# Attention scores against block keys: one matmul for both query halves, and another form of filler matmul

## The chip, the cores and the metric

One core of a Trainium2 chip runs the whole program. Its TensorE (PE in the rows) multiplies a stationary matrix, loaded as weights (PEld), with a stream of moving columns and writes to PSUM. VectorE (DVE), ScalarE (ACT) and GpSimd (POOL) work on PSUM and SBUF, and SyncE (SP) issues the loads and stores. The metric is the device time of one execution in microseconds (us). Three runs of the kernel before took 647.77, 648.09 and 649.55 us; their median is 648.09.

## What is computed

Three stages follow each other. The first is attention with 2 batches of 8 heads, 768 positions and 64 dimensions a head. Every query sees the keys that lie less than 16 positions away, and besides them 24 block keys, one for each block of 32 positions (the maximum over the block's keys; its value is the block's mean). The second and third are two feed-forward networks on the 1536 x 512 result.

```python
k_sum = k.reshape(B, H, nb, block, D).max(axis=3)      # nb = 24 blocks of 32
v_sum = v.reshape(B, H, nb, block, D).mean(axis=3)
scores_l = scale * np.matmul(q, k.transpose(0, 1, 3, 2))        # masked to |i - j| < 16
scores_s = scale * np.einsum('bhsd,bhnd->bhsn', q, k_sum) + np.log(block)
a = softmax(concat([masked scores_l, scores_s]))
x = a @ concat([v, v_sum])
# then
x = rmsnorm(x) * rms_g ; x = (silu(x @ w_gate) * (x @ w_val)) @ w_out
out = (s * relu(x @ w_in)**2 + b) @ w_out2
```

## The kernel before, in words

The queries are cut into 12 tiles of 128 positions, 6 for each batch. A head pair (NPAIR = 4 of them) lies on the 128 partitions: head g = 0 on partitions 0 to 63, head g = 1 on 64 to 127, with the 64 dimensions of a head as rows. A tile's 128 queries are two halves of 64, c = 0 and c = 1, since each half has a window of KW = 96 keys of its own: its 64 positions and 16 on either side. The NS = 24 block keys (`km`) are the same for both halves. So the scores of one head and one tile are 128 queries x KC = 120 columns, 96 of the window and 24 of the blocks, and four heads of them fill one PSUM bank; `box["S", i, g]` is the bank of tile i and of the heads g of all four pairs.

`do_qk` (L510 to L523) writes the scores of a tile. For each pair j it issues four matmuls of 64 x 64 weights and 96 columns for the window, one for each (g, c), and then four of 64 x 64 weights and 24 columns for the block keys. The queries are the weights, with 64 rows (the dimensions of one head) and 64 columns (the queries of one half); the output goes to partitions 0 to 63 or 64 to 127 of the bank. All operands are float32, and each such matmul appears in the profile as two rows, two passes; a tile of scores is 4 x 8 x 2 = 64 rows of L522.

After the scores, VectorE adds the mask and takes the minimum of the negated scores (`do_top`, L541), ScalarE exponentiates (L548), TensorE transposes the result (L559), ScalarE copies it to SBUF (L569), and TensorE multiplies with the values (L578, 120 x 64 weights, 66 columns). Norms, another transposition (L627) and the split of x into a high and a low part (L638, L640) follow. The block keys come from L284, the block sums of the values from L294, their transposition from L299.

The order of this stage is made by a planner, `give_out` (L328 to L417). It goes through a model of time with a cost for each task (1.25 us for a tile's scores, 0.44 for four transposes), and issues on each engine the first task by rank whose inputs are there in the model. Where the model's TensorE would stand idle for more than IDLE = 0.6 us, it issues a filler into a free PSUM bank: four transposes of the identity matrix (L413 and L414), which the model counts as 0.44 us and whose result nobody reads. The first matmuls of the feed-forward network (L726, L727, L730, in the halves and in float32r) are tasks of the same planner; from some 115 us on the plain loops of `moe` run. The order that the planner finds is what the program has; on the chip each engine goes through its own list and waits on semaphores.

Of the kernel before, what the change touches and what calls it, by code (L numbers as in the profile page):

```python
# [24 lines left out]
NS = SEQ // BLK  # L25
HQ = 64
VH = 66
KW = HQ + 2 * WIN
KC = KW + NS
# [13 lines left out]
QB = 3  # L43
# [11 lines left out]
def kernel(ctx: ExitStack, tc: tile.TileContext, q_t, k_t, v_w, v_t, w_gate, w_val, w_out, w_in2, w_out2, vecs, out):  # L55
    nc = tc.nc
# [40 lines left out]
    def bank(i):  # L97
        return psp.tile([128, 512], F32, tag=f"b{i}", name=f"b{i}")


    ident = const.tile([128, 128], F32, name="ident")
# [7 lines left out]
    qc = [const.tile([128, NPAIR, 2, HQ], F32, name=f"q{i}") for i in range(QB)]  # L109
# [13 lines left out]
    kst = [t[:, 0:NPAIR * KL].rearrange("p (j s) -> p j s", j=NPAIR) for t in kb]  # L123
    vst = [[t.rearrange("p (s h d) -> p s h d", s=NTL, h=NH) for t in ts]
           for ts in ([t[:, 0:VT] for t in vb], [part[:, i * VT:(i + 1) * VT] for i in range(2)])]
    km = [const.tile([128, NPAIR, NS], F32, name=f"km{b}") for b in range(NB)]
# [192 lines left out]
    def task(eng, us, fn, deps=(), rank=0.0, take=(), give=(), bank=None, free=(), more=0.09):  # L319

        t = dict(eng=eng, us=us, fn=fn, deps=[d for d in deps if d is not None], rank=rank, take=take, give=give,
                 bank=bank, free=free, more=more, end=None)
        tasks.append(t)
        return t
# [3 lines left out]
    def give_out():  # L328
        count = {k: 0 for k in rings}
        freed = {k: 0 for k in rings}  # L330
        done_at = {k: [] for k in rings}
        bank_free = [(0.0, i) for i in range(8)]
        used_caps = {k: [] for k in caps}
        pending = {e: [] for e in ("PE", "DVE", "ACT", "POOL", "SP")}
        for i, t in enumerate(tasks):
            pending[t["eng"]].append((t["rank"], i, t))
        for p in pending.values():
            p.sort(key=lambda z: z[:2])
        clock = dict.fromkeys(pending, 0.0)
        dma = 0.0  # L340
        now = 0.0
        left = len(tasks)

        ends = {k: {} for k in rings}

        def ring_ok(k):
            n = rings[k]
            c = count[k]
            return c < n or (c - n in ends[k] and ends[k][c - n] <= now)

        while left:
            moved = False
            for e in ("SP", "PE", "ACT", "DVE", "POOL"):
                if clock[e] > now + 1e-9:
                    continue
                for z in pending[e]:
                    t = z[2]
                    if any(d["end"] is None or d["end"] + LAT > now + 1e-9 for d in t["deps"]):
                        continue
                    if not all(ring_ok(k) for k in t["take"]):  # L360
                        continue
                    b = None
                    if t["bank"]:
                        if sum(1 for x in used_caps[t["bank"]] if x["freed"] is None or x["freed"] > now) >= caps[t["bank"]]:
                            continue
                        ok = [x for x in bank_free if x[0] <= now]
                        if not ok:
                            continue
                        b = min(ok)
                        bank_free.remove(b)  # L370
                        t["b"] = b[1]
                        t["freed"] = None
                        used_caps[t["bank"]].append(t)
                    t["slot"] = {}
                    for k in t["take"]:
                        t["slot"][k] = count[k]
                        count[k] += 1
                    if e == "SP":
                        dma = max(dma, now + 0.5) + t["us"]
                        clock[e] = max(now + 0.06, dma - AHEAD)  # L380
                        t["end"] = dma + 1.3
                    else:
                        clock[e] = now + t["us"]
                        t["end"] = clock[e] + (0.06 if e == "PE" else t["more"])
                    for k, o in t["give"]:
                        ends[k][o["slot"][k]] = t["end"] + LAT
                    for o in t["free"]:
                        o["freed"] = t["end"] + LAT
                        bank_free.append((o["freed"], o["b"]))
                    t["at"] = now  # L390
                    if b is not None:
                        t["fn"](b[1])
                    else:
                        t["fn"]()
                    pending[e].remove(z)
                    left -= 1
                    moved = True
                    break
            if moved:
                continue  # L400
            nxt = [c for c in clock.values() if c > now + 1e-9]
            nxt += [x[0] for x in bank_free if x[0] > now]
            nxt += [v for k in rings for v in ends[k].values() if v > now]
            nxt += [t["end"] + LAT for t in tasks if t["end"] is not None and t["end"] + LAT > now + 1e-9]
            assert nxt, [z[2]["why"] if "why" in z[2] else (e, z[0]) for e in pending for z in pending[e][:3]]
            now = min(nxt) + 1e-6
            at = clock["PE"] + IDLE
            if now > at and any(x[0] <= at for x in bank_free) and ident_at[0]["end"] is not None and ident_at[0]["end"] + LAT < at and pending["PE"]:

                now = at  # L410
                i = min(bank_free)[1]
                ps = bank(i)
                for k in range(4):  # L413
                    nc.tensor.transpose(ps[:, k * 128:(k + 1) * 128], ident, ident)  # L414
                clock["PE"] = now + 0.44

    def dve(n):  # L417
        return 0.07 + 1.042e-3 * n
# [10 lines left out]
    def plan(x):  # L429
# [12 lines left out]
        def lq(i, rank, deps=()):  # L442
            Q[i] = task("SP", mb(128 * 512 * 4), lambda: load_q(i), deps, rank=rank)
# [60 lines left out]
        box = {}  # L504
        def tile_of(n, i):
            b, t = divmod(i, NTL)
            if i >= 2:
                lq(i, n - 5, [qk[i - QB]] if i >= QB else ())

            def hold(bk):  # L510
                box["S", i, 0] = bank(bk)

            def do_qk(bk):
                box["S", i, 1] = bank(bk)
                sm_of[i] = smallp.tile([128, 2, NH], F32, tag="sm", name="sm")
                four = [(g, c) for g in range(2) for c in range(2)]
                for j in range(NPAIR):
                    for o, n in ((0, KW), (KW, NS)):
                        for g, c in four:
                            p = slice(64 * g, 64 * g + 64)  # L520
                            k0 = 64 * (2 * t + c)
                            nc.tensor.matmul(box["S", i, g][64 * c:64 * c + 64, j * KC + o:j * KC + o + n], qc[i % QB][p, j, c],  # L522
                                             km[b][p, j] if o else kst[b][p, j, k0:k0 + KW], start=True, stop=True)  # L523
            deps = [Q[i], *[KM[b, j] for j in range(NPAIR)], *([qk[i - 1]] if i else ())]
            A0 = task("PE", 0.0, hold, deps, n + 1.2, bank="S")
            A1 = qk[i] = task("PE", 1.25, do_qk, [*deps, A0], n + 1.2, bank="S", take=("sm",))
            box["A0", i] = A1
            return A0, A1

        for n, (i, g) in enumerate(us):  # L530
            b, t = divmod(i, NTL)
# [86 lines left out]
            S = task("POOL", 0.75, do_ss, [R], n - 2)  # L618
# [50 lines left out]
        for s in range(NSUB):  # L669
            for j in range(HEAD):  # L670
                rk = FR[s] + j * FS
                got = {}
                for k in range(2):
                    ps = []
# [38 lines left out]
                c = task("DVE", dve(512), lambda f=do_v: f(0), [b_, got[1][2]], rr, free=(got[1][0],))  # L713
# [153 lines left out]
    x = [xs0]  # L867
    plan(x)
    give_out()
    n = 2 * HEAD + MORE  # L870
    prog[:] = [n, n, n, n]
# [71 lines left out]
```

## Time and profile before

| | |
|---|---|
| median of three runs | 648.09 us |
| the profiled execution's own time | 647.01 us |
| its span, first to last instruction | 645.2 us |
| TensorE busy | 622.8 us, 97% of the span, 3816 matmul rows |
| VectorE, ScalarE, GpSimd busy | 378.1, 259.8, 141.7 us |
| mean granted TensorE clock | 0.992 |
| score matmuls, 96 columns (384 rows) | 277 ns mean of one |
| score matmuls, 24 columns (384 rows) | 208 ns mean of one |
| filler transposes (52 rows) | 327 ns mean of one |

A row's duration is its latency, from the start to the last result, and rows overlap: eight rows of 24 columns that take some 0.2 us each are through in 0.08 us. What a group costs TensorE is therefore read from start to start, not from the durations. "Busy" of an engine in a stretch is the part of it in which at least one of its rows runs. The column PEclk is the granted clock of TensorE as a share of full speed (1.00 is 2.4 GHz, 0.50 is 1.2 GHz). In the chain of waits "issue" is time in which an engine waited for nothing that the profile shows.

### The profile page before, as it was taken

How to read it: one execution, taken by the hardware profiler on the slowest of the kernel's cores; microseconds unless marked ns; L12 is line 12 of the kernel's file. 1: busy time of each engine (PE TensorE's matmuls, PEld its weight loads, DVE VectorE, ACT ScalarE, POOL GpSimd, SP SyncE). 2: the span in 40 equal slices, each digit the busy share in tenths (PEclk: the TensorE clock that was granted, in tenths of full speed). 3: DMA queues.
4: the chain of work that ended last, by engine and by line, in shares of the span. 5: the costliest groups of instructions: out<-in, count | busy, mean ns of one | idle time of the engine just before them, and what ended most of it. 6: DMA issues, size and time to landing. Idle time of an engine off the chain costs nothing.

```text
span 645.2 us, 9632 instructions
## 1 busy us (share of the span) xinstructions
PE 622.8 (97%) x3816; PEld 514.3 (80%) x3816; DVE 378.1 (59%) x731; ACT 259.8 (40%) x524; POOL 141.7 (22%) x159
## 2 busy tenths in 40 slices
PE   5588999999999999999999999999999999999998
PEld 3576788888888888888888888888888888888886
DVE  5469886325851555544556767870388457845532
ACT  2576986334433333212333345542554045404400
POOL 2253856322311111111111111100221022103100
PEclk9889999999999999999999999999999999999999
DMA  9979622003440112221122212230212321210022
GB/s 294 230 264 257 193 60 74 1 1 98 131 130 28 42 63 66 86 61 53 62 65 69 64 65 67 65 100 31 56 46 67 94 62 42 66 61 0 2 98 99
DMA packets 17494, 55.04 MB, mean 85 GB/s; under 512 B 2000, under 2 KB 2256, under 8 KB 17448
## 3 DMA queue, kind: packets, MB, share of 16 engines
q1 hardware_dynamic: 17448, 54.42, 27.7%
q8 instruction: 30, 0.49, 0.3%
q14 instruction: 16, 0.13, 0.1%
HBM read 50.35 MB, written 3.15 MB: 83 GB/s over the span
## 4 chain that ended last, share of the span: by engine, by line
PE 91%; DVE 3%; issue 2%; DMA 1%; ACT 1%; SPq 0%; POOL 0%; POOLq 0%
PE b L726 22%; PE b L730 22%; PE b L727 22%; PE b L852 7%; PE b L850 7%; PE b L849 7%; PE b L559 2%; PE b L522 2%; PE b L578 2%; DMA vt<-in_v_t_dram 1%; PE b L627 1%; DVE vt L294 1%; DVE P L541 0%; DVE km L284 0%; ACT P L548 0%
## 5 line engine op out<-in xcount | busy, mean ns | idle before, releaser
L231 POOL TENSOR_TENSOR wl<-wa,wh 128x512 fp32r<-128x512 f32 x68 | 89.1, 1318 | 389.3 <-ACT wh L227 316.0
L726 PE MATMUL b<-x,wh 128*128 128x512 f32 x288 | 113.7, 395 | 0.1
L727 PE MATMUL b<-x,wl 128*128 128x512 f32 x288 | 112.2, 390 | 0.0
L227 ACT ACTIVATE wh<-wa 128x512 fp32r<-128x512 f32 x68 | 41.5, 627 | 97.2 <-PE b L852 45.5
L730 PE MATMUL b<-x,wh 128*128 128x512 f32 x288 | 77.8, 392 | 0.0
L850 PE MATMUL b<-wl,hg 128*128 128x512 f32 (+1 forms) x196 | 75.1, 385 | 0.0
L849 PE MATMUL b<-wh,hg 128*128 128x512 f32 (+1 forms) x196 | 75.1, 385 | 0.0
L726 PE MATMUL b<-y,wh 128*128 128x512 f32 x192 | 74.7, 389 | 0.0
L727 PE MATMUL b<-y,wl 128*128 128x512 f32 x192 | 74.7, 389 | 0.0
L831 DVE SCALAR_TENSOR_TENSOR b<-u,vec 128x512 f32<-128x512 f32 x48 | 50.7, 1057 | 35.6 <-ACT u L830 35.6
L726 PEld LDWEIGHTS b<-x,wh 128*128 128x128 f32 x288 | 54.1, 188 | 11.3 <-ACT x L638 0.4
L727 PEld LDWEIGHTS b<-x,wl 128*128 128x128 f32 x288 | 54.1, 188 | 10.7
L730 PEld LDWEIGHTS b<-x,wh 128*128 128x128 f32 x288 | 53.5, 188 | 11.0
L726 PE MATMUL b<-hg,wh 128*128 128x512 f32 x144 | 56.0, 389 | 0.0
L727 PE MATMUL b<-hg,wl 128*128 128x512 f32 x144 | 56.0, 389 | 0.0
L751 DVE SCALAR_TENSOR_TENSOR hg<-b,vec,hg 128x512 fp32r<-128x512 f32 x48 | 36.0, 749 | 28.1 <-ACT hg L750 28.1
L852 PE MATMUL b<-wh,hg 128*128 128x512 f32 (+1 forms) x196 | 51.5, 385 | 0.0
L730 PE MATMUL b<-y,wh 128*128 128x512 f32 x192 | 51.3, 389 | 0.0
L216 DVE SCALAR_TENSOR_TENSOR wa<-raw,wa 128x512 int32<-128x512 int32 x68 | 50.0, 735 | 2.0
L750 ACT ACTIVATE hg<-b,vec 128x512 fp32r<-128x512 f32 x48 | 33.0, 687 | 43.0 <-DVE b L831 43.0
L858 DVE TENSOR_TENSOR part<-b,part 128x512 f32<-128x512 f32 (+1 forms) x37 | 24.4, 673 | 43.5 <-PE b L852 43.5
L215 DVE SCALAR_TENSOR_TENSOR wa<-raw,wa 128x512 int32<-128x512 int32 x68 | 47.0, 691 | 2.0
(85 smaller groups left out, 947.2 us busy)
## 6 DMA issues: line engine op xcount, KB each, us to landing
raw<-in_w_out_dram SPq DMA_DIRECT2D x28, 512.0 KB, 3.5
raw<-in_w_in_dram SPq DMA_DIRECT2D x16, 512.0 KB, 4.1
raw<-in_w_gate_dram SPq DMA_DIRECT2D x12, 512.0 KB, 3.6
raw<-in_w_val_dram SPq DMA_DIRECT2D x12, 512.0 KB, 3.6
hg<-in_k_t_dram SPq DMA_DIRECT2D x8, 400.0 KB, 10.0
q<-in_q_t_dram SPq DMA_DIRECT2D x12, 256.0 KB, 7.1
vt<-in_v_t_dram SPq DMA_DIRECT2D x8, 384.0 KB, 8.3
out_dram<-part SPq DMA_DIRECT2D x11, 256.0 KB, 2.0
```

The source lines that it names most:

```text
L215: lambda: nc.vector.scalar_tensor_tensor(out=ai, in0=hi, scalar=-0x80000000, in1=ai, op0=ALU.bitwise_and, op1=ALU.bitwise_or),
L216: lambda: nc.vector.scalar_tensor_tensor(out=ai, in0=lo, scalar=29, in1=ai, op0=ALU.logical_shift_right, op1=ALU.bitwise_or),
L227: nc.scalar.activation(out=r(h), in_=a_t[i], func=AF.Copy)
L231: nc.gpsimd.tensor_tensor(out=r(lo), in0=a_t.pop(i), in1=high[i], op=ALU.subtract)
L726: nc.tensor.matmul(ps, r(hi[:, kk * 128:(kk + 1) * 128]), xh, start=kk == 0, stop=False)
L727: nc.tensor.matmul(ps, r(lo[:, kk * 128:(kk + 1) * 128]), xh, start=False, stop=False)
L730: nc.tensor.matmul(ps, r(hi[:, kk * 128:(kk + 1) * 128]), r(act(kk, 1)), start=False, stop=kk == 3)
L751: nc.vector.scalar_tensor_tensor(out=r(dst[1]), in0=ps, scalar=bias, in1=dst[0], op0=ALU.add, op1=ALU.subtract)
L831: after(0, lambda u=u, ps=ps: nc.vector.scalar_tensor_tensor(out=ps, in0=u, scalar=sbc[:, 0:1], in1=u, op0=ALU.mult, op1=ALU.mult))
L849: nc.tensor.matmul(acc, gh, r(ws[e][0][:, cs]), start=e == 0, stop=False)
L850: nc.tensor.matmul(acc, gh, r(ws[e][1][:, cs]), start=False, stop=False)
L852: nc.tensor.matmul(acc, r(ge[e][:, 1]), r(ws[e][0][:, cs]), start=False, stop=e == 3)
```

## The change

There are two edits. The scores of the block keys are no longer computed once for each half of the queries: the two halves of a head stand side by side as 128 columns of one set of weights (64 rows x 128 columns), and one matmul of 24 columns writes all 128 partitions of the bank. A pair then has four window matmuls of 64 x 64 as before, and two block matmuls of 64 x 128, so a tile has 4 x (8 + 4) = 48 rows for 64. A filler is one float32 matmul of the identity with 256 columns, the identity taken twice, in place of four transposes: two rows for four. The planner's costs are as before, so its order is as before.

```diff
@@ give_out
                 ps = bank(i)
-                for k in range(4):
-                    nc.tensor.transpose(ps[:, k * 128:(k + 1) * 128], ident, ident)
+                nc.tensor.matmul(ps[:, 0:256].rearrange("p (o c) -> p o c", o=2), ident, ident.rearrange("p (o c) -> p o c", o=1).broadcast_to([128, 2, 128]), start=True, stop=True)
                 clock["PE"] = now + 0.44
@@ do_qk
-                four = [(g, c) for g in range(2) for c in range(2)]
                 for j in range(NPAIR):
-                    for o, n in ((0, KW), (KW, NS)):
-                        for g, c in four:
-                            p = slice(64 * g, 64 * g + 64)
+                    for g in range(2):
+                        p = slice(64 * g, 64 * g + 64)
+                        S = box["S", i, g]
+                        for c in range(2):
                             k0 = 64 * (2 * t + c)
-                            nc.tensor.matmul(box["S", i, g][64 * c:64 * c + 64, j * KC + o:j * KC + o + n], qc[i % QB][p, j, c],
-                                             km[b][p, j] if o else kst[b][p, j, k0:k0 + KW], start=True, stop=True)
+                            nc.tensor.matmul(S[64 * c:64 * c + 64, j * KC:j * KC + KW], qc[i % QB][p, j, c], kst[b][p, j, k0:k0 + KW], start=True, stop=True)
+                    for g in range(2):
+                        p = slice(64 * g, 64 * g + 64)
+                        nc.tensor.matmul(box["S", i, g][:, j * KC + KW:(j + 1) * KC], qc[i % QB][p, j].rearrange("p c q -> p (c q)"), km[b][p, j], start=True, stop=True)
```

The lists of VectorE, ScalarE, GpSimd and SyncE hold the same instructions in the same order before and after; on TensorE 96 places and 13 fillers differ. The first place is on TensorE, in the tile of scores that stands behind 69 us between two halves of a feed-forward matmul (in the kernel before it starts at 86.35 us). A row gives the line, the operation, the tile written, the tiles read, and weight columns x moving columns; `hg` holds the keys, `q` the queries, x2 stands for the two halves. Before:

```order
L726 MATMUL b_1377<-x,wh 128x512
L727 MATMUL b_1377<-x,wl 128x512
L522 MATMUL b_1376<-hg,q_100 64x96 x2
L522 MATMUL b_1392<-hg,q_100 64x96 x2
L522 MATMUL b_1376<-km_110,q_100 64x24 x2
L522 MATMUL b_1392<-km_110,q_100 64x24 x2
L522 MATMUL b_1376<-hg,q_100 64x96 x2
```

The same place after:

```order
L727 MATMUL b_1258<-x,wh 128x512
L728 MATMUL b_1258<-x,wl 128x512
L521 MATMUL b_1257<-hg,q_100 64x96 x2
L521 MATMUL b_1273<-hg,q_100 64x96 x2
L524 MATMUL b_1257<-km_110,q_100 128x24
L524 MATMUL b_1273<-km_110,q_100 128x24
L521 MATMUL b_1257<-hg,q_100 64x96 x2
```

The window matmuls stand where they stood; behind them come two block matmuls of 128 weight columns instead of four of 64, in each of the four pairs.

The second place is on TensorE too, between the scores of tile 0 and those of tile 1: the first four fillers, the transposes of tile 0 (`P`), and those of the value sums (`vt`). Before:

```order
L522 MATMUL b_155<-km_109,q_99 64x24 x2
L414 MATMUL b_193<-ident 128x128 x4
L414 MATMUL b_206<-ident 128x128 x4
L414 MATMUL b_216<-ident 128x128 x4
L414 MATMUL b_229<-ident 128x128 x4
L559 MATMUL b_237<-ident,P 120x128 x4
L559 MATMUL b_243<-ident,P 120x128 x4
L299 MATMUL b_250<-ident,vt 128x128 x4
```

The same place after:

```order
L524 MATMUL b_155<-km_109,q_99 128x24
L413 MATMUL b_185<-ident 128x256
L413 MATMUL b_195<-ident 128x256
L413 MATMUL b_202<-ident 128x256
L413 MATMUL b_212<-ident 128x256
L560 MATMUL b_217<-ident,P 120x128 x4
L560 MATMUL b_223<-ident,P 120x128 x4
L299 MATMUL b_230<-ident,vt 128x128 x4
```

Each filler is one matmul in place of four transposes, and nothing else moved.

## Rows read from the trace of the kernel before

**Rows 1.** Windows: busy us (xinstructions) of PE, PEld, DVE, ACT, POOL; PEclk, DMA, GB/s

```profile
42.00:69.00 27.00, 22.89 (x381) 18.50 (x381) 25.87 (x68) 20.13 (x53) 13.70 (x18) 1.00 0.79 216
69.00:645.00 576.00, 573.04 (x2960) 474.05 (x2960) 330.44 (x568) 220.34 (x418) 115.73 (x104) 1.00 0.21 64
```

**Rows 2.** Chain that ended last, in order of time: start us, us, what

```profile
20.60 2.25 issue
...
28.26 4.58 issue
...
40.70 0.84 issue
...
69.00 0.69 PE b L578 x16
```

**Rows 3.** Windows between the stops, columns as in rows 1

```profile
0.00:20.61 20.61, 13.30 (x222) 10.20 (x222) 11.46 (x35) 6.88 (x16) 4.87 (x25) 1.00 0.93 288
...
22.85:28.29 5.44, 5.41 (x125) 4.86 (x126) 2.86 (x22) 3.03 (x10) 0.94 (x4) 0.69 1.04 169
...
32.84:40.71 7.87, 7.65 (x126) 6.40 (x125) 4.78 (x26) 6.08 (x19) 3.63 (x6) 0.74 1.03 387
```

**Rows 4.** DMA queues, 30 to 32 us: packets, MB, share of engines

```profile
q8 instruction: 1, 0.02, 4.2%
```

**Rows 5.** Page, part 3: DMA queues, whole span

```profile
q8 instruction: 30, 0.49, 0.3%
```

**Rows 6.** Windows around the slow clock, columns as in rows 1

```profile
23.26:26.67 3.41, 3.41 (x60) 3.02 (x56) 2.13 (x17) 1.79 (x5) 0.32 (x2) 0.50 1.08 171
...
30.08:36.91 6.83, 4.06 (x35) 3.48 (x35) 2.02 (x11) 2.28 (x7) 1.01 (x1) 0.50 1.03 327
```

**Rows 7.** Windows, line L522 alone: us, PE, PEld, PEclk, DMA, GB/s

```profile
69.00:115.00 46.00, 5.40 (x256) 4.98 (x256) 1.00 0.30 90
```

**Rows 8.** Timeline of PE, one tile: start us, us, what, shape, type, count

```profile
85.80 0.39 PE L726 MATMUL b<-x,wh 128*128 128x512 f32 x1
86.02 0.40 PE L727 MATMUL b<-x,wl 128*128 128x512 f32 x1
86.35 0.40 PE L522 MATMUL b<-hg,q 64*64 64x96 f32 x8
86.57 0.26 PE L522 MATMUL b<-km,q 64*64 64x24 f32 x8
86.65 0.38 PE L522 MATMUL b<-hg,q 64*64 64x96 f32 x8
...
87.41 0.26 PE L522 MATMUL b<-km,q 64*64 64x24 f32 x8
87.60 0.50 PE L726 MATMUL b<-x,wh 128*128 128x512 f32 x1
87.94 0.40 PE L727 MATMUL b<-x,wl 128*128 128x512 f32 x1
```

**Rows 9.** Timeline of PEld, same place, columns as in rows 8

```profile
85.80 0.19 PEld L727 LDWEIGHTS b<-x,wl 128*128 128x128 f32 x1
86.35 0.15 PEld L522 LDWEIGHTS b<-hg,q 64*64 64x64 f32 x4 [0.36 <-issue]
```

**Rows 10.** Line L414, the fillers: ns min/median/max, first and last start

```profile
L414 PE MATMUL b<-ident x52: 272/273/474, 10.1 to 70.0; 128*128 128x128 f32 x52
```

**Rows 11.** Timeline of PE, first stage

```profile
14.87 1.81 PE L559 MATMUL b<-ident,P 128*120 128x128 f32 x8
16.52 0.60 PE L299 MATMUL b<-ident,vt 128*128 128x128 f32 x4
...
25.63 0.60 PE L522 MATMUL b<-hg,q 64*64 64x96 f32 x8
...
37.24 0.40 PE L522 MATMUL b<-hg,q 64*64 64x96 f32 x8
```

**Rows 12.** Timeline of ACT: the last exponentials of tile 1

```profile
20.79 1.81 ACT L548 ACTIVATE P<-P,sm 128x120 f32<-128x120 f32 x6
```

## The prediction

> **What bounds the kernel now.** I read the stretches first. From 69 us to the end TensorE is the bound: it is busy for 573.04 of the 576 us there, VectorE for 330.44 [rows 1]. Whatever the change adds to TensorE's own work behind 69 us is added to the time. From 42 to 69 us VectorE is the bound (25.87 of 27 us), and TensorE stands idle for 4.1 [rows 1]. Before 42 us I read the chain of waits. Beside loads it holds three stops of TensorE that no semaphore ends, put down to "issue": 2.25 us at 20.60, 4.58 at 28.26, 0.84 at 40.70 [rows 2]. Their places tell what they are. TensorE ran 222 matmul rows up to the first, 125 from there to the second, 126 to the third [rows 3]. Each row is a weight load and a matmul, so the stops lie some 250 instructions apart. A packet of the instruction queue moves between 30 and 32 us, shortly ahead of the end of the longest stop [rows 4], and the queue's packets are some 16 KB each (0.49 MB in 30) [rows 5]; the DMA engines are full meanwhile (shares of 0.93 to 1.04) [rows 3]. So I read the stops as TensorE waiting for its own code behind the loads. The stops also cost clock: the granted clock was 0.50 from 23.26 to 26.67 and from 30.08 to 36.91, each time after a stretch in which TensorE had stood still [rows 6]. At 69.00 the chain enters TensorE and stays there [rows 2].
>
> So two things count: what a tile of scores costs TensorE behind 69 us, and how much earlier or later TensorE gets there.
>
> **The change part by part.**
>
> *The block columns, behind 69 us.* 256 score rows run there, four of the 12 tiles [rows 7]. The tile at 86.35 takes 1.25 us until the next matmul at 87.60: four head pairs, each 8 rows of 96 columns (86.35 to 86.57, 0.22 us) and 8 rows of 24 (86.57 to 86.65, 0.08 us) [rows 8]. The 64x64 matmuls run four at a time, so the rows that the change removes are the cheapest that there are: 0.08 us a pair, 1.3 us over four tiles. In their place stand 4 rows of 64x128. What no row shows is a step from 64x64 to 64x128 and back. The nearest rows are the other changes of tile size. From 128x128 to 64x64: 86.02 to 86.35 is 0.33, where two 128-wide matmuls lie 0.22 apart: +0.11. Back: the last 24-column block takes 0.19 (87.41 to 87.60) for 0.08, +0.11, and the first 128-wide matmul after it takes 0.34 for 0.23, +0.11 for weights that weren't there [rows 8]. The weight loads show why: inside one size the next weights start 0.22 us ahead of their matmul (85.80 for 86.02); across a change they start with it, at 86.35, 0.36 us after the engine's weight side went idle [rows 9]. It reads as if the array is emptied first.
>
> The Trainium skill, TensorEngine Tiling (Array Packing), Key Properties, says that a change of tiling mode, and not of the tile alone, drains TensorE. The rows above agree for changes that involve all 128 rows; whether 64x64 to 64x128 counts, which share the split of the rows, none shows. By the rule the forecast of 649.3 us holds, without it the rival of 645.8.
>
> With emptying: a tile has seven more changes (two for each of four pairs, less the exit that it pays now): 7 x 0.10 = 0.70. One exposed load of 128-wide weights a pair and 0.02 for its columns (24, where 72 more columns in two passes make a block 0.14 longer), for the 0.08 removed: 4 x (0.11 + 0.02 - 0.08) = 0.20. Together +0.90 a tile, 2.15 for 1.25. Bounds: with both passes' weights exposed 0.70 + 4 x (0.22 - 0.08) = 1.26; with no emptying and half the rows, 4 x -0.04 = -0.16. I take 0.90, since every change of size in these rows pays, that of columns (L578, 128x64) as that of rows. Four tiles: **+3.6 us** (-0.6 to +5.0).
>
> *The block columns from 42 to 69 us.* Three tiles get 0.90 longer there, beside 4.1 us of idle TensorE while VectorE is the bound; its score work waits for nothing of theirs today. I charge **+0.3** (0 if the cover holds, 2.7 if none does).
>
> *The fillers.* Four transposes of 128 columns stream 512 columns, the new matmul two passes of 256: the same. There are 13 of them (52 transposes, the last at 70.0 us) [rows 10], issued where TensorE would wait; I cost them at 0. The first ones stand right in front of the score transposes of 14.87 [rows 11]; if a second load of weights stood open in each of the first four, at half clock twice 0.11, these would start 0.9 later; the clock rival below, -0.8, is the bound on the other side. A filler before tile 8 lies on the chain: two weight loads in place of four, 0 too.
>
> *Fewer rows, so the code stops move.* A tile has 48 rows for 64, a filler 2 for 4. Counting 222 rows in the new order: tile 0 (48), four fillers (8), transposes (8), means (4), tile 1 (48), values (32), tile 2 (48), transposes (8) make 204; the first stop comes 18 rows into tile 3 and not inside tile 2. Those transposes need the exponentials that end at 22.60 [rows 12]; at full clock they are through near 23.4, where tile 3 begins, instead of at 25.63 [rows 11]. Row 222 is then reached near 24. The piece of code, which came at 22.86, is asked for about 1 us later (28 rows into tile 1, and that tile is longer), so it comes at 24 to 25.4. Of the first stop 0 to 1.4 us is left; tile 3 ends at 25.4 to 26.8, not at 27.3. The next 125 rows end 35 rows into tile 4 instead of in the values before it. Its code took 10 us after the previous piece (22.86 to 32.85), so it comes near 34 to 35.4, and tile 4, which began at 37.24 [rows 11] and was through 1.25 later, is through at 35 to 37: 1.5 to 3.5 earlier. The third stop, 0.84, moves to the end of tile 5, where the loads have thinned out. I take **-2.7 us** (0, if the code comes as late as TensorE gets faster, to -4.5). From there VectorE's same list of work starts earlier, and so does all behind it.
>
> **The sum:** 3.6 + 0.3 + 0 - 2.7 = +1.2 us. The profiled execution took 647.01 us (span 645.2), 1.08 under the median of 648.09; so about 648.2 for it, and **649.3 us** by the median. I call a difference under 0.3% (1.9 us) one that measurement can't tell from none.
>
> **Rivals.**
> *No emptying between 64x64 and 64x128.* The rows stay split in two halves, and only columns join. For it: no row shows this step. Against: 128x64 to 128x128 also joins only columns, and its next weights are not preloaded either. A tile then costs about +0.1; 0.4 - 2.7 = -2.3: 645.8 us.
> *The code stops don't shrink* (slower). The emptying costs TensorE its 0.9 in tiles 1 to 4 as well, the pieces of code come as much later as they are asked for later, and the DMA engines are as full as before. The 2.7 falls away, and 3.6 + 0.3 remain: 652.0 us. It decides from the point where tile 4 is through no earlier than 38.5. For it: the code comes at the pace of the loads; against: 48 rows of work for 64 lie in each piece.
> *The clock rises earlier.* The transposes of the first fillers run at up to 474 ns, where 273 is the median [rows 10]; at 16.52 four others take 0.60, the pace of full clock, and between there were only transposes [rows 11]. If matmuls raise the clock one step earlier, the eight rows at 14.87 take half of 1.81: -0.8 on the sum, 648.5 us. The Trainium skill, TensorE: Matmul & The Clock Gate, Part 4: PE-mode transpose, says that transposes do not engage the full clock; in this trace it rose after nothing but transposes, so I give that little.
>
> **How the numbers follow.** Forecast with emptying and part of the stops regained: 0.47, and its own range is 647.5 to 651.5 (tile 0.7 to 1.26, gain 1.5 to 4). No emptying: 0.23. Stops not shrinking: 0.25. Clock: 0.05. The lower end of the range reaches the second case, 645.4; the upper the third, 652.8. Faster by over 0.3% (under 646.1): more than half of the second case and a few hundredths of the others, 0.20. Slower (over 650.0): the third case and some three tenths of the first, 0.37. Within: 0.43.
>
> **What would show it.** In the changed kernel's rows one tile behind 69 us: 2.0 to 2.4 us with weights starting with their matmul at each step to L524 says emptying; 1.2 to 1.4 with preloaded weights says none. The "issue" rows of the chain: sum well under 7.7 us, the first behind 23 us, the second in a tile of scores. The time at which TensorE's idle ends for good: 66 to 67 us for 69.0. The clock: one half-speed stretch less between 23 and 37 us. If that time doesn't move, the third case holds; if the tile stays near 1.3, the second.

## The result and the profile after

The changed kernel takes 652.22 us (median of 6 runs, 651.06 to 654.05), the kernel before 648.49 (6 runs, 647.77 to 649.55): ratio 1.0062, 95% interval 1.0046 to 1.0079. It is slower, by 3.7 us. The forecast was 649.3. The time lies in the whole range given (645.4 to 652.8), near its upper end, and outside the range of the likeliest case alone (647.5 to 651.5).

The profiled execution took 652.76 us (span 650.98, before 645.20). One table tells where the 5.78 us between the spans lie. The columns come from TensorE's timeline: the time at which tile 4's scores are through, from there to the start of tile 8 (the first of the four late tiles), the part of this that lies before the start of tile 5, and from the start of tile 8 to the end.

| kernel | tile 4 through | to tile 8 | of it to tile 5 | to the end | span |
|---|---|---|---|---|---|
| before | 38.49 | 31.72 | 6.87 | 574.99 | 645.20 |
| after | 36.21 | 34.21 | 7.78 | 580.56 | 650.98 |
| difference | -2.28 | +2.49 | +0.91 | +5.57 | +5.78 |

So, in these two profiles, the early part wins what was foreseen, the middle gives it back, and the four late tiles cost more than was charged. Of the middle's 2.49, 0.91 lies ahead of tile 5, where no changed scores stand, and 1.58 between the starts of tiles 5 and 8.

The windows of after, in the columns of [rows 1]: TensorE's idle time from 42 to 69 us has shrunk from 4.11 to 1.46 us, and behind 69 us it is still the bound.

```profile
42.00:69.00 27.00, 25.54 (x298) 18.79 (x296) 25.52 (x71) 18.81 (x48) 13.61 (x19) 1.00 0.80 230
69.00:651.00 582.00, 578.66 (x2894) 477.19 (x2894) 329.92 (x564) 220.71 (x419) 114.64 (x102) 1.00 0.20 63
```

The chain of after, for [rows 2]: one stop put down to "issue" is left of three, 0.86 us for 7.67, and the chain stays in TensorE from 69.17, not earlier than before.

```profile
33.73 0.86 issue
...
69.17 0.34 PE b L579 x4
```

The windows for [rows 3] and [rows 6]: 346 rows up to the stop, and one stretch at clock 0.50 (34.22 to 41.04), of which TensorE now works 6.40 us, where in the longer one before it worked 4.06 of as many.

```profile
0.00:33.74 33.74, 26.91 (x346) 19.53 (x346) 19.04 (x81) 16.56 (x48) 10.53 (x36) 1.00 0.97 262
...
34.22:41.04 6.82, 6.40 (x52) 4.90 (x54) 2.82 (x15) 2.65 (x8) 1.14 (x2) 0.50 1.03 395
...
17.15:34.22 17.07, 16.28 (x286) 12.97 (x284) 9.81 (x57) 13.10 (x40) 7.04 (x13) 1.00 1.04 241
```

The slow stretch has moved with the stop. Most of it now lies behind tile 4, where the kernel before ran at full clock and had its third stop instead. The two parts of the middle, first before (from 38.49), then after (from 36.21):

```profile
38.49:45.36 6.87, 5.46 (x79) 4.21 (x73) 5.42 (x19) 6.18 (x20) 3.89 (x7) 1.00 0.70 270
45.36:70.21 24.85, 21.10 (x357) 17.10 (x357) 24.47 (x70) 18.11 (x47) 13.05 (x18) 1.00 0.86 230
```

```profile
36.21:43.99 7.78, 7.41 (x69) 5.29 (x67) 5.72 (x20) 5.37 (x15) 2.80 (x5) 0.69 0.93 360
43.99:70.42 26.43, 25.12 (x297) 18.79 (x297) 24.49 (x70) 18.24 (x47) 13.44 (x19) 1.00 0.82 230
```

A late tile in TensorE's timeline, for [rows 8]: from 89.35 to 91.99, 2.64 us for 1.25. A block of eight window rows takes 0.32, 0.22 before; a block of four block-key rows takes 0.34, where eight took 0.08.

```profile
89.02 0.40 PE L728 MATMUL b<-x,wl 128*128 128x512 f32 x1
89.35 0.40 PE L521 MATMUL b<-hg,q 64*64 64x96 f32 x8
89.67 0.41 PE L524 MATMUL b<-km,q 64*128 64x24 f32 x4
90.01 0.40 PE L521 MATMUL b<-hg,q 64*64 64x96 f32 x8
90.33 0.41 PE L524 MATMUL b<-km,q 64*128 64x24 f32 x4
...
91.65 0.41 PE L524 MATMUL b<-km,q 64*128 64x24 f32 x4
91.99 0.50 PE L727 MATMUL b<-x,wh 128*128 128x512 f32 x1
```

The weight side at the same place, for [rows 9]: at each step the weights start with their own matmul (89.34, 89.67, 90.00, 90.33), never under the matmuls ahead, and the four loads of 64x128 keep the weight side for 0.30 of the block's 0.34.

```profile
89.34 0.21 PEld L521 LDWEIGHTS b<-hg,q 64*64 64x64 f32 x8 [0.37 <-issue]
89.67 0.30 PEld L524 LDWEIGHTS b<-km,q 64*128 64x128 f32 x4
90.00 0.21 PEld L521 LDWEIGHTS b<-hg,q 64*64 64x64 f32 x8
90.33 0.30 PEld L524 LDWEIGHTS b<-km,q 64*128 64x128 f32 x4
```

The first stage, for [rows 11]: the score transposes start 1.00 later (15.87 for 14.87). Tile 3 (25.30) begins 0.33 earlier than before and runs through without a stop until 27.95. The stop lies inside tile 4, which is through at 36.21.

```profile
10.66 5.06 PE L413 MATMUL b<-ident 128*128 128x256 f32 x8
15.87 1.67 PE L560 MATMUL b<-ident,P 128*120 128x128 f32 x8
...
17.91 0.40 PE L521 MATMUL b<-hg,q 64*64 64x96 f32 x8
...
25.30 0.40 PE L521 MATMUL b<-hg,q 64*64 64x96 f32 x8
...
27.95 1.15 PE L579 MATMUL b<-hg,PT 120*64 120x66 f32 x32
...
34.58 0.62 PE L524 MATMUL b<-km,q 64*128 64x24 f32 x2 [0.86 <-issue]
...
36.21 1.15 PE L579 MATMUL b<-hg,PT 120*64 120x66 f32 x16
```

### The profile page after: what moved, and what is told of

Its sections match the earlier page's. It is cut to its first block, busy times and chain, and to the rows that moved or that the text cites. A ratio compares the mean times of both kernels' runs of the same rounds, so it can differ in the third digit from the quotient of the medians.

```text
span 651.0 us, 9196 instructions
## 1 busy us (share of the span) xinstructions
PE 638.5 (98%) x3598; PEld 521.3 (80%) x3598; DVE 378.2 (58%) x731; ACT 260.0 (40%) x524; POOL 140.5 (22%) x159
## 4 chain that ended last, share of the span: by engine, by line
PE 97%; DMA 1%; ACT 1%; issue 0%; DVE 0%; POOL 0%; SPq 0%
PE b L727 22%; PE b L731 22%; PE b L728 22%; PE b L853 7%; PE b L850 7%; PE b L851 7%; PE b L524 3%; PE b L521 2%; PE b L579 2%; PE b L560 2%; PE b L413 1%; PE b L628 1%; DMA hg<-in_k_t_dram 1%; ACT PT L570 0%; POOL sm L591 0%
```

## The experiments

All were timed in five rounds, with runs of the kernel before between them on the same chip (medians 648.6 for the first four, 648.05 for the next four, 647.8 for the last); times below are medians, and differences are to that kernel. In the expectations E stands for the theory that each change of tile size empties TensorE, W for the rival that the wide weights alone cost, C for the earlier clock. This table has the columns of the one above, each from the profiled execution, which is not always near the median: for the scores alone it took 649.19 us (3.1 under), for the fillers alone 649.99 (2.9 over).

| kernel | tile 4 through | to tile 8 | of it to tile 5 | to the end | median | ratio, 95% interval |
|---|---|---|---|---|---|---|
| grouped | 35.96 | 31.59 | 7.17 | 577.30 | 646.91 | 0.9980 (0.9961 to 1.0000) |
| 48 rows, one size | 34.24 | 30.48 | 5.93 | 575.00 | 643.19 | 0.9916 (0.9891 to 0.9942) |
| scores only | 34.61 | 32.23 | 5.87 | 580.57 | 652.29 | 1.0080 (1.0050 to 1.0110) |
| fillers only | 41.90 | 31.32 | 6.78 | 575.00 | 647.09 | 0.9976 (0.9952 to 1.0000) |
| new in tiles 8 to 11 | 39.31 | 31.79 | 6.13 | 580.59 | 653.27 | 1.0080 (1.0058 to 1.0102) |
| new in tiles 0 to 4 | 35.66 | 32.71 | 7.07 | 574.99 | 645.66 | 0.9975 (0.9951 to 0.9998) |
| grouped in tiles 0 to 4 | 37.44 | 32.07 | 7.53 | 575.00 | 646.51 | 0.9968 (0.9952 to 0.9984) |
| new in tiles 5 to 7 | 40.30 | 32.36 | 5.93 | 574.98 | 649.25 | 1.0024 (1.0011 to 1.0037) |
| grouped in tiles 0 to 7 | 36.71 | 31.55 | 7.11 | 575.00 | 644.22 | 0.9947 (0.9923 to 0.9970) |

**Grouped.** The same matmuls, but all window rows of a tile ahead of all block rows: one change of size inside a tile for seven.

```diff
                         for c in range(2):
                             k0 = 64 * (2 * t + c)
                             nc.tensor.matmul(S[...], qc[i % QB][p, j, c], kst[b][p, j, k0:k0 + KW], ...)
+                for j in range(NPAIR):
                     for g in range(2):
                         p = slice(64 * g, 64 * g + 64)
                         nc.tensor.matmul(box["S", i, g][:, ...], qc[i % QB][p, j]..., km[b][p, j], ...)
```

> The changed kernel, but a tile issues the window matmuls of all four pairs first and then the block matmuls of all four: the same rows, two changes of tile size a tile in place of eight. Theory E (each change of size empties TensorE for some 0.09 us, and 128-wide float32 weights stand open): the tile behind 69 us falls from 2.64 to 1.8 to 2.0 us, four tiles give 2.6 to 3.4, and the time is 648.5 to 649.5 against 652.2 for the changed kernel. Rival W (the two weight loads of 128 columns are the whole cost, a change of size costs nothing): the number of loads is the same, so the tile stays at 2.5 to 2.65 and the time at 652.

A tile takes 1.83 us (84.85 to 86.68 in its timeline): the windows 0.82, the block rows 1.01.

```profile
84.85 0.89 PE L521 MATMUL b<-hg,q 64*64 64x96 f32 x32
85.67 1.08 PE L525 MATMUL b<-km,q 64*128 64x24 f32 x16
86.68 0.50 PE L728 MATMUL b<-x,wh 128*128 128x512 f32 x1
```

So 0.81 of the 1.39 belongs to the six changes that are gone (0.135 each): E holds. (That rows of 96 and of 24 columns take turns is not the cost: they do so in the kernel before too, at one size, in 1.25 us a tile.) But 0.58 is left with one added change. The block rows go in 8 pairs of halves, of which each takes 0.11 (8 x 0.11 and 0.11 for the way back are the 1.01); four pairs of heads took 4 x 0.08 [rows 8]. If its one change costs 0.135 like the six, 0.44 a tile is the price of the wide weights. The Trainium skill, TensorE: Matmul & The Clock Gate, LDWEIGHTS (loading the stationary operand), gives a weight load its number of columns over 1.2 in ns, whatever the rows; that makes, as an estimate, 107 for 128 columns and 53 for 64. The 0.11 a step agrees: the block rows run at the pace of their weights. The time came out 2 us under the expectation; the late part (577.30, 2.3 over the kernel before) is a little under the 2.6 to 3.4 expected, and the early one is better.

**48 rows of one size.** The new count of rows without a change of size. Left out: the second half's block-key scores; its window is 24 columns wider instead.

```diff
                 for j in range(NPAIR):
+                    for g, c in ((0, 0), (0, 1), (1, 0), (1, 1)):
+                        p = slice(64 * g, 64 * g + 64)
+                        w = KC if c else KW
+                        k0 = min(64 * (2 * t + c), KL - w)
+                        nc.tensor.matmul(box["S", i, g][64 * c:64 * c + 64, j * KC:j * KC + w], qc[i % QB][p, j, c],
+                                         kst[b][p, j, k0:k0 + w], start=True, stop=True)
                     for g in range(2):
                         p = slice(64 * g, 64 * g + 64)
...
-                        nc.tensor.matmul(box["S", i, g][:, ...], qc[i % QB][p, j]..., km[b][p, j], ...)
+                        nc.tensor.matmul(box["S", i, g][0:64, ...], qc[i % QB][p, j, 0], km[b][p, j], ...)
```

> 48 rows a tile as in the changed kernel, all of them 64x64: the second half of the queries gets one window matmul of 120 columns, so its 24 block scores are left out (24 more window columns stand in their place); the fillers are the new ones. No change of size inside a tile. Theory E: a tile behind 69 us takes 1.15 to 1.35 as before; the code stops before 42 us shrink as in the changed kernel (one stop under 1.5 us in place of 7.7 in three), and the time is 645.5 to 647.0, 1.5 to 3 under the kernel before. Rival N (the code comes later by what TensorE is faster): stops of some 7 us remain and the time is 648 to 649.

5.4 us less, more than expected: tile 4 is through 4.25 earlier and the middle is 1.2 shorter. In its chain the stops at the places of the first two are 0.85 and 1.03 us, for 2.25 and 4.58 [rows 2]. One stop under 1.5 us was expected; it has these two and, in its timeline, 0.30 ahead of 30.42 and 0.75 ahead of 42.17, 2.9 us together for 7.67.

```profile
24.64 0.85 issue
...
32.70 1.03 issue
```

So fewer rows do pay at the code stops, here nearly up to the bound given (-4.5). With the changed form the late tiles take it back.

**Scores only, fillers only.** Each half of the change alone.

```diff
-                nc.tensor.matmul(ps[:, 0:256]..., ident, ident..., start=True, stop=True)
+                for k in range(4):
+                    nc.tensor.transpose(ps[:, k * 128:(k + 1) * 128], ident, ident)
```

> The new scores with the old fillers (four transposes). Theory E: the fillers matter for less than 0.5 us, the time is 651.5 to 653. Rival F (the new fillers, at half clock 1.28 us each for 1.17, are a good part of the loss or of the early gain): the time differs from the changed kernel's 652.2 by more than 1.5 us.

> The new fillers with the old scores. Theory E: within 1 us of the kernel before; 26 rows less move the code stops by a few rows only. Rival F: more than 1.5 us away from it. Rival C (matmuls as fillers raise the clock earlier): the clock is up one step earlier than 16.4 us and the time is about 0.8 lower.

The scores alone give 652.29, the changed kernel's time. The fillers alone give 647.09, 1.5 under the kernel before. E had said within 1 us and F more than 1.5 away, and this lies at F's border; but its interval reaches 1.0000, and beside the new scores the fillers change nothing (652.29 and 652.22). They are free, or gain a little. Their chain has the long stops of before (these two are its rows), and the clock rose at 19.95 in their profile, at 16.43 before, so the rival of the earlier clock falls.

```profile
22.60 4.29 issue
...
32.29 3.68 issue
```

**New form in the late tiles alone.**

```diff
+                if i >= 8:
                     (the new form)
+                else:
                     (the old form)
```

> Form of the change for the scores of tiles 8 to 11 alone (the four behind 69 us); tiles 0 to 7 keep the old scores, and the fillers are the new ones. Theory (the late tiles are the loss: 1.39 us each, where the prediction said 0.90): 647.1 (new fillers alone) + 4 x 1.39 = 652.7 us, a tile behind 69 us takes 2.64 us, and everything up to 69 us reads as with the new fillers alone. Rival (the loss is made early, and the late tiles' length is partly covered): 647 to 649.5 us.

653.27, 5.2 us over the kernel before, with late tiles of 2.64 us (90.05 to 92.70 in the timeline) and 580.59 us behind the start of tile 8, 5.6 more than with old ones. Nothing covers the late tiles: their extra length stands in the time in full, and no gain of the early part stands against it.

**New form in tiles 0 to 4 alone, and grouped there.** As above with `if i < 5:`; the second has the grouped form in its place.

> Form of the change for tiles 0 to 4 alone, old scores from tile 5 on, new fillers. Theory (fewer rows early win time at the code stops, which the longer tiles 5 to 7 and 8 to 11 then eat): 644.5 to 646.5 us, the first stop gone, the second in tile 4 (row 346), and TensorE without idle from about 66 to 67 us. Rival (the early part wins nothing, since the longer tiles 1 to 4 eat it themselves): 647 us or more.

> As the run before, but in tiles 0 to 4 all window matmuls of the four head pairs come first and then all block matmuls: two changes of tile size a tile instead of eight. Theory: the same rows in each piece of code and about 0.8 us less for each tile that lies on the path: 643 to 645 us, less than either kernel. Rival (the pieces of code set the early part, not the length of the tiles): the same as the run before, within 1 us.

645.66 and 646.51 us: both beat the kernel before, by 2.4 and 1.5, the first only just by its interval, and they don't differ from one another by what these intervals can tell. The theory for the second falls: its tile 2 is 0.8 shorter (1.83 for 2.65), but TensorE comes to the second piece of code 1.0 earlier and waits longer for it, and the piece comes 1.1 later (35.61 for 34.51, the ends of these stops). First the chain of the ungrouped, then of the grouped one:

```profile
34.12 0.39 issue
```

```profile
33.09 2.52 issue
```

Both stop at row 346. In these two, the pieces of code set the early pace and not the length of a tile.

**New form in tiles 5 to 7 alone.** `if 5 <= i < 8:`.

> Form of the change for tiles 5 to 7 alone (the three between 42 and 69 us), old scores elsewhere, new fillers. The prediction charged these three with +0.3, hidden beside VectorE: 647.1 to 647.6 us and TensorE without idle from the same time as with the new fillers alone. Rival (they are on the path there, which the traces of the changed kernel suggest): 3 x 1.39 = up to 4.2 more, 649 to 651 us.

649.25: 1.2 over the kernel before, where the fillers alone are 1.5 under it: 2.7 us for three tiles that are 4.2 longer together, so they are not hidden, though intervals of 1.6 and 0.8 us either way leave the size open. Its waits of TensorE from 42 to 73 us sum to 1.5 us; with the old form there are 3.7. First the new form, then the fillers alone (columns: who waited for whom, us, times, longest):

```profile
PE b L589 <- ACT PT L580: 1.5, 4, 0.5
```

```profile
PE b L577 <- ACT PT L568: 1.6, 3, 0.7
PE b L626 <- DVE xn L618: 1.4, 2, 0.9
PE b L577 <- POOL ss L615: 0.7, 1, 0.7
```

The 2.2 us of waits that went are the part that was covered; what is longer than that is on the path. The profiles set the size: from the start of tile 5 to that of tile 8 it takes 26.43 us here and 24.54 with the fillers alone, so 1.89 of the 4.2 is on the path.

**Grouped in tiles 0 to 7, old form behind.** `if i < 8:` with the grouped form.

> Grouped form (all window matmuls of a tile, then all block matmuls) for tiles 0 to 7, old scores for tiles 8 to 11, new fillers. Grouped everywhere stood 1.7 us under the kernel before although its four late tiles cost 4 x 0.58 = 2.3 us; if the late tiles are all that it pays, leaving them old gives 1.7 + 2.3 = 4.0 under it, 644 to 645 us, with TensorE without idle from about 67.5 us. Rival (tiles 5 to 7 are on the path and pay 0.58 each, and the lead of the grouped run was a matter of the clock's phase): as with tiles 0 to 4 alone or up to 1.7 above it, 646.5 to 648.2 us.

644.22 us, 3.6 under the kernel before: less than both kernels, and the lowest median of the versions that compute the whole. Tiles 5 to 7 take 1.83 there (52.91 to 54.73), and old tiles stand from 68.26 on, 1.95 earlier than before.

```profile
52.91 0.89 PE L522 MATMUL b<-hg,q 64*64 64x96 f32 x32
53.73 1.07 PE L526 MATMUL b<-km,q 64*128 64x24 f32 x16
54.73 0.50 PE L742 MATMUL b<-x,wh 128*128 128x512 f32 x1
...
68.26 0.43 PE L534 MATMUL b<-hg,q 64*64 64x96 f32 x6
```

From the start of tile 5 to that of tile 8 it takes 24.44, as the old form does (24.85): 3 x 0.58 is hidden, and 3 x 1.39 was only in part. Its chain still stops twice:

```profile
26.61 0.95 issue
...
34.00 1.71 issue
```

## Why the prediction was right or wrong

The forecast was the likeliest case, within 0.3%; the kernel is slower by more than that. The mechanism of its largest term was right, its size was not, and one cost had no term: the slow clock behind tile 4.

*The late tiles, +3.6: mis-sized, 5.57 measured.* TensorE does empty between 64x64 and 64x128 (0.135 us a change, and weights that start with their matmul), so the rival without emptying falls. The Trainium skill, TensorEngine Tiling (Array Packing), Key Properties, had said that a change of tiling mode drains TensorE; with 0.135 us a change the traces agree for this step too. Two steps failed, in equal parts: "One exposed load of 128-wide weights a pair", and the price of a change. The forecast charged 4 x 0.05 for block rows and weights and 7 x 0.10 for the changes, 0.90; measured are 4 x 0.11 and 7 x 0.135, together 1.39 (0.24 a tile more for the weights, 0.25 for the changes). Each of the two f32 passes waits for weights of its own, 0.11 a time. The bound with both exposed stood in the text as 1.26, and even that was passed. The 0.10 had been read off changes with 128x128 on one side; why one costs more between 64x64 and 64x128 no run tells. The end that I set aside was the better one.

*The middle tiles, +0.3: wrong, +1.58 in the profile, +1.89 in the run with the new form in these tiles alone.* The cover of 4.1 us of idle time was read as free, but that idle time is waits for single results, in certain places; only what falls into such a wait is hidden. Between the starts of tiles 5 and 8 TensorE was idle for 3.75 us before and still is for 1.31, so some 2.4 to 2.6 us of the 4.2 of added rows are covered. The measured term lies under the bound without cover, 3 x 0.90.

*A term left at nothing: the clock behind tile 4, +0.91.* The text had noted that the stops cost clock, and put no price on where the slow stretch would come to lie. It came from 34.22 to 41.04; from the end of tile 4 to the start of tile 5 TensorE works at 0.50 for 4.83 of 7.78 us, where before it took 6.87 with a stop of 0.84. That the clock is the cost, the other profiles show: at a clock of 1.00 throughout and without a stop, this stretch takes 5.87 to 6.13 (scores only, 48 rows, new in tiles 8 to 11, new in tiles 5 to 7), with a slow stretch in it 6.78 to 7.53. The rows of the scores alone, which have the form of the changed kernel (columns as in [rows 1]):

```profile
34.61:40.48 5.87, 5.27 (x74) 4.18 (x72) 5.40 (x19) 5.11 (x15) 3.01 (x5) 1.00 1.03 397
```

*The code stops, -2.7: right at the end of tile 4, -2.28; at the start of tile 5 the clock has left -1.37 of it.* The row at which each piece of code ends was counted to a row: the stop came after 346 rows, 347 were forecast, in tile 4 as said. That tile was to be through 1.5 to 3.5 earlier. The first stop is gone, not for the reason given: row 222 was to be reached near 24 and was reached near 26 (tile 3 starts at 25.30, its 18th row lies in its second pair), since tile 1 starts 0.86 later (17.91 for 17.05) and tiles 1 and 2 take 2.65 each, 0.5 over the forecast. The code's packet, for [rows 4], moves between 22 and 24 us here, and between 20 and 22 before; first after, then before:

```profile
q8 instruction: 1, 0.02, 3.7%
```

```profile
q8 instruction: 1, 0.02, 4.0%
```

So two errors offset one another: the stop is gone because TensorE itself was late. The third, 0.84, is gone too. That the stops wait for code, the traces bear out further than the prediction did: wherever TensorE stops after 220 to 222, 346 or 347, or 471 to 473 rows, 19 times in ten profiles, it goes on 1.2 to 1.7 us after the end of such a packet of 16 KB (in the changed kernel at 34.58, after a packet that ends at 33.06).

*The fillers, 0: right* by their own run. The four in front of the transposes take 5.21 us until these start (10.66 to 15.87), 4.8 before (10.1 in [rows 10] to 14.87 in [rows 11]): 0.11 each, half of the bound set. (The other 0.57 of the 1.00 is tile 0, whose scores are through that much later.) The clock rose at 17.15, no earlier than at 16.43 before, and between 17.25 and 21.22 in the other profiles with the new fillers: that rival is out. (Where the text says that it rose after nothing but transposes, that holds from 10.1 on; ahead of them ran the score matmuls of tile 0.) The stretch of before:

```profile
16.43:23.26 6.83, 4.37 (x157) 3.87 (x158) 3.44 (x19) 4.63 (x14) 2.24 (x4) 1.00 1.04 256
```

*The rival of code stops that don't shrink* named the time, 652.0, by the wrong way: its condition, tile 4 not through before 38.5, was not met (36.21). That the range reached up to the measured time was luck, since only this rival carried it there. The sum by measured terms is -2.28 + 0.91 + 1.58 + 5.57 = +5.78 on the span. That the medians differ by 3.7 is because the profiled execution of before lies 1.5 under its median (648.49), and that of after 0.5 over. The late part is the same in every profile of a form (580.56 to 580.59 with the new one, 574.98 to 575.00 with the old); so, as an estimate from these, all that stands ahead of tile 8 wins some 1.8 us by the medians, while in this pair of profiles it loses 0.2.

Of the signs named, tile length (2.0 to 2.4, was 2.64), the issue sum and the stop in a tile of scores came out so or stronger. Of two slow stretches one is left, as said, but it lies later, from 34.22 to 41.04. TensorE's last idle time was to end at 66 to 67 and ended at 69.17: the clock behind tile 4 and the middle tiles took back what the stops had won.

## What to carry to other kernels

Count what a merged matmul does to its neighbours: fewer rows are worth nothing if each one stands between rows of another tile size, and rows that stream few columns run at the pace of their weights. If such a merge is wanted for the instruction count, sort it so that the size changes once, and use it only where the engine waits for code or data anyway. Idle time of an engine covers only work that falls into that very wait: before it is booked as cover, name the waits one by one. And where a stop moves, look at the clock as well: in this kernel the slow stretch moved with it, onto work that had run at full clock.

## What the runs showed of the hardware

- A change between 64x64 and 64x128 costs TensorE 0.135 us at full clock (0.81 for six), though both split the rows in two halves.
- Two f32 weight loads of 64x128, one for each half of the rows, go side by side, a pair every 0.11 us (grouped: eight pairs in 1.01 us with the way back); 24 columns of matmul hide nothing of that.
- The stops for code come after 220 to 222 and after 346 or 347 matmul rows, whatever the rows are, in two profiles (before, 48 rows) after 471 to 473 too; the changed kernel and the new or grouped form in tiles 0 to 4 alone have only the second, and the profile of the scores alone has none. How long they last reads as a race of TensorE with the packet: the second piece cost 0.39 us with the new form in tiles 0 to 4, 0.86 in the changed kernel, 1.71 to 2.53 with the grouped form there, 2.38 to 4.58 with the old one. The packet itself ended between 31.2 and 34.6 us from profile to profile, with one and the same form too (31.4 to 34.6 with the old one), so a single profile does not rank the forms.
- Not explained: with the scores alone three of twelve runs took 657.3 to 657.9 us, at a mean clock of 1.00, while the others took 649.2 to 653.6; none of the three was profiled. With the new form in tiles 0 to 4, two of twelve took 651.1 and 651.3 us, the others 642.8 to 647.0.
